# One load of 128 rows, its source read twice, in place of two loads of 64 rows, for the queries and keys of heads 12 to 63 in a fused attention and mixer kernel

## The chip, the core and the metric

The kernel runs on one core of one Trainium2 chip. The metric is device time in microseconds (us) of one execution, the median over runs. Engines go by the profile's names: PE (TensorE matmul), PEld (its weight loads), DVE (VectorE), ACT (ScalarE), POOL (GpSimd) and SP (SyncE, whose queue issues every transfer here). A *transfer* is one DMA instruction; it moves its rows as packets on the core's 16 DMA engines.

## The reference

Eight sequences of 576 tokens with 8 heads of width 64 go through block-causal attention (blocks of 64), and the result goes through a mixing layer of rank 32 along the sequence and a two-layer network of width 2048.

```
scores = scale * np.matmul(q, k.transpose(0, 1, 3, 2))     # (8, 8, 576, 576), scale = 1/8
mask = block_i >= block_j                                  # blocks of 64 positions
scores = np.where(mask, scores, -1000000000.0)
attn = softmax(scores)                                     # row sum + 1e-9
x = matmul(attn, v)                                        # heads side by side: (8, 576, 512)
h = x.T @ U @ V                                            # along the sequence, rank 32
u = x + h.T
out = u + np.maximum(u @ w_ch1, 0.0) @ w_ch2               # 512 -> 2048 -> 512
```

The kernel gets queries and keys as one array `qk` of shape (64, 64, 1152): for each of the 64 heads, 64 rows (the width), 576 columns of queries and then 576 of keys, so a row is 4,608 bytes and a head 288 KB.

## The kernel before, in words

**What runs over what.** The outer loop goes over 64 heads, head 0 to head 63. For each head the kernel loads q and k, forms the scores tile by tile (`softmax`, five row tiles of 64 or 128 queries), takes row maxima on DVE (L968) and exponentials on ACT (L979), normalises on POOL (L1005), transposes the weights on PE (L1038), splits them into high and low parts (ACT L1015, DVE L1057) and multiplies them with v on PE (L1097). After every second head `mix` applies the rank-32 layer and writes a piece of u to DRAM (L1166). The two-layer network of the first half of the weights (`ffn_chunk`: PE L465 and L488) is laid between the heads, one batch behind; after the last head comes the second half (`block_products`, PE L659).

**Queries and keys of a head.** `split_qk` loads into `raw`, a ring of two tiles of 128 x 1152, so head h uses `raw[h % 2]`. Up to head 11 only rows 0 to 63 are loaded (L868) and the scores are taken in plain fp32 (L950). From head FS = 12 on the scores are taken in two matmuls of fp32r (L954, L955), which need high and low parts, and both halves of `raw` get the same 64 rows: L868 fills rows 0 to 63, L873 fills rows 64 to 127. Then, in this order:

- ACT casts the queries of all 128 rows to q1 (L889), scales the keys in place (L892) and casts them to k1 (L894).
- POOL subtracts the low part of the queries in rows 64 to 127 (L896) and that of the keys in rows 0 to 63 into k2 (L900).
- SP copies rows 0 to 63 of q1 to q2 by a transfer (L904, 144 KB).
- PE takes the scores from q1, k1, q2, k2 (L954, L955).

`raw[h % 2]` is free for head h + 2 when L900 of head h is done, and the load of head h + 2 waits for that on SP.

**What sets the order.** A planner (`Plan.issue`) simulates the five engines as queues: each task has an engine, a cost in ns, a priority, and buffers that it reads and writes. It hands out ring buffers as they come free in its own simulated time and writes the instructions of every engine in the order in which the simulated engines took them up. A transfer costs its task's ns on SP, and its data count as there 3,000 ns later (`DL`). Before the change the load of heads 12 to 63 is entered at 1640 ns for its two transfers (L882). On the chip each engine works through that fixed order, and an instruction whose data are late holds up all that stands behind it on its engine.

**The other transfers.** All go through SP's one queue: v for two heads (`vr`, L913), pieces of u written (L1166) and read back for the network (`ur`, L440), its results (`o_d`, L499; read back at L452 and, in the second half, as `whole`), the weights (`st`, L372 and L387), and the final result (L756).

Of the kernel before, what the change touches and what calls it, by code (L numbers as in the profile page):

```python
# [16 lines left out]
P = 128  # L17
# [29 lines left out]
FS = 12  # L47
# [6 lines left out]
NEAR, DL = 130, 3000  # L54
# [83 lines left out]
class Plan:  # L138
# [8 lines left out]
    def add(self, engine, ns, prio, fn, reads=(), writes=(), hold=(), after=0, port=False):  # L147

        n = len(self.tasks)
        deps = set()  # L150
        for b in reads:
            deps.update(b.writers)
            b.readers.append(n)
        for b in hold:
            deps.update(b.readers, b.writers)
        for b in writes:
            deps.update(b.readers, b.writers)
            b.writers, b.readers = [n], []
        deps.discard(n)
        slots = {b for b in (*reads, *writes) if b.pool is not None}  # L160
        for b in slots:
            b.users += 1
        self.tasks.append((engine, ns, prio, fn, deps, after, slots, port or engine == "POOL"))
# [76 lines left out]
def _act(n, sbuf=False):  # L240
    return (93 if sbuf else 52) + 0.833 * n


def _dve(n):
    return 69 + 1.042 * n
# [9 lines left out]
def attention_then_mixer(  # L255
# [10 lines left out]
    nc = tc.nc  # L266
# [8 lines left out]
    add = plan.add  # L275

    def f32(ap):
        return ap.bitcast(F32)
# [531 lines left out]
    for r in raw_r:  # L810
# [3 lines left out]
        for x, fill in ((qi, 1.0), (ki, NEG)):  # L814
            nc.gpsimd.affine_select(
                out=x[:, :, 1, :], in_=x[:, :, 1, :], pattern=[[-1, 4], [0, 64]], compare_op=ALU.not_equal,
# [46 lines left out]
    def split_qk(h, pr):  # L863
        raw, q1, k1, q2, k2 = (r[h % 2] for r in (raw_r, q1_r, k1_r, q2_r, k2_r))

        def fetch():
            if h:
                nc.sync.dma_start(out=raw[0:64, :], in_=qk[h])  # L868
            else:
                for a in (S, 0):  # L870
                    nc.sync.dma_start(out=raw[0:64, a : a + S], in_=qk[h, :, a : a + S])
            if h >= FS:
                nc.sync.dma_start(out=raw[64:P, :], in_=qk[h])  # L873

        if h in (FS - 2, FS - 1):

            for n, (x, o) in enumerate(((q2, 0), (k2, S))):
                add(
                    "DVE", _dve(S) / 2, pr, lambda x=x, o=o: nc.vector.tensor_copy(x[64:P, :], raw[64:P, o : o + S]),
                    [raw], [x],  # L880
                )
        add("SP", 1640 if h >= FS else 820, pr, fetch, writes=[raw], after=DL)  # L882
        if h < FS:
            add(
                "ACT", _act(S, True), pr,
                lambda: nc.scalar.activation(raw[0:64, S : 2 * S], raw[0:64, S : 2 * S], AF.Copy, scale=SCALE), [raw], [raw],
            )
            return
        add("ACT", _act(S, True), pr, lambda: nc.scalar.copy(q1.ap, raw[:, 0:S]), [raw], [q1])  # L889
        add(  # L890
            "ACT", _act(S, True), pr,
            lambda: nc.scalar.activation(raw[:, S : 2 * S], raw[:, S : 2 * S], AF.Copy, scale=SCALE), [raw], [raw],  # L892
        )
        add("ACT", _act(S, True), pr, lambda: nc.scalar.copy(k1.ap, raw[:, S : 2 * S]), [raw], [k1])  # L894
        add(
            "POOL", 1380, pr, lambda: nc.gpsimd.tensor_sub(q1[64:P, :], raw[64:P, 0:S], f32(q1[64:P, :])),  # L896
            [raw, q1], [q1],
        )
        add(
            "POOL", 1380, pr, lambda: nc.gpsimd.tensor_sub(k2[0:64, :], raw[0:64, S : 2 * S], f32(k1[0:64, :])),  # L900
            [raw, k1], [k2],
        )

        add("SP", 600, pr, lambda: nc.sync.dma_start(out=f32(q2[0:64, :]), in_=f32(q1[0:64, :])), [q1], [q2], after=DL)  # L904
# [265 lines left out]

    wa = weight_tiles(wp, 0)
    split_qk(0, 0.0)
    split_v(0, 2.0)
    mixing_weights(MP)
    wab = weight_bufs()
    load_w1(lambda: wa, 0, wab, lambda n: WP0 + WP1 * n, (0,))
    for h in range(NH):
        pr = 1000.0 * h
        if h + 1 < NH:
            split_qk(h + 1, max(pr - LA, 1.0))  # L1180
        for g, tiles in ((1, (4, 3)), (0, (2, 1, 0))):
            for x in ((4,), (3,)) if g else ((2,), (1, 0)):
                softmax(h, x, pr + 10)
            normalise(h, tiles, pr + 10)
        for g in (1, 0):
            for part in range(2):
                transpose(h, g, part, pr + 20 + 10 * (1 - g))
            apply_v(h, g, pr + 30)
        if h + 1 < NH:
            split_v(h + 1, pr + 1000)  # L1190
        if h % 2 == 1:
            mix(h // 2, pr + 40)
        if h == min(WH, NH - 1):
            gate = Buf()
            gate.writers = [len(plan.tasks) - 1]
            load_w2(lambda: wa, 0, wab, lambda n: WPB + WP1 * n, [gate], ks=range(FH))
            load_w1(lambda: wa, 0, wab, lambda n: WP2 + WP3 * n, (1,), [gate])
            load_w2(lambda: wa, 0, wab, lambda n: WP4 + WP3 * (n - FH), [gate], ks=range(FH, FC))
# [59 lines left out]
```

## Time and profile before

| | |
|---|---|
| median of 3 runs | 1185.89 us (1184.37 to 1186.47) |
| profiled execution: time of the run | 1188.18 us |
| profiled execution: span | 1186.4 us |
| busy: PE, PEld | 1164.9 us (98%), 1132.5 us (95%) |
| busy: DVE, ACT, POOL | 937.9 us (79%), 775.6 us (65%), 455.2 us (38%) |
| transfers of q and k | 115 of 288 KB, 2 of 144 KB |
| busy share of the 16 DMA engines by SP's queue | 38.2% of the span |
| data moved | 130.36 MB, 110 GB/s on the mean |

The run's time is 1.8 us above the span, which begins with the first and ends with the last instruction of the program. A busy share is an average over stages: the heads last until about 635 us, and the network's second half follows. PE at 98% means that it has hardly any idle time; that its matmuls are at their peak is not said. The DMA share is a mean over 16 engines and does not tell how a transfer is divided among them.

### The profile page before, as it was taken

How to read it: one execution, taken by the hardware profiler on the slowest of the kernel's cores; microseconds unless marked ns; L12 is line 12 of the kernel's file. 1: busy time of each engine (PE TensorE's matmuls, PEld its weight loads, DVE VectorE, ACT ScalarE, POOL GpSimd, SP SyncE). 2: the span in 40 equal slices, each digit the busy share in tenths (PEclk: the TensorE clock that was granted, in tenths of full speed). 3: DMA queues.
4: the chain of work that ended last, by engine and by line, in shares of the span. 5: the costliest groups of instructions: out<-in, count | busy, mean ns of one | idle time of the engine just before them, and what ended most of it. 6: DMA issues, size and time to landing. Idle time of an engine off the chain costs nothing.

```text
span 1186.4 us, 25102 instructions
## 1 busy us (share of the span) xinstructions
PE 1164.9 (98%) x8988; PEld 1132.5 (95%) x8988; DVE 937.9 (79%) x2008; ACT 775.6 (65%) x1924; POOL 455.2 (38%) x582
## 2 busy tenths in 40 slices
PE   8989989999999999999999999999999999999998
PEld 7777989999999999999999999999999999999998
DVE  6898877878788877777877587326989889889887
ACT  7888878898888889988887352214544444444443
POOL 5656867675667676767664112110000000000000
PEclk9999999999999999999999999999999999999999
DMA  4455665544544444445431433211242142142121
GB/s 139 146 149 151 186 163 156 139 127 128 135 120 124 132 127 129 117 123 143 127 107 56 132 121 123 86 46 55 61 121 70 51 121 67 56 120 64 58 81 41
DMA packets 75868, 130.36 MB, mean 110 GB/s; under 512 B 8928, under 2 KB 52960, under 8 KB 75744
## 3 DMA queue, kind: packets, MB, share of 16 engines
q1 hardware_dynamic: 75744, 128.76, 38.2%
q8 instruction: 71, 1.16, 0.4%
q14 instruction: 53, 0.43, 0.1%
HBM read 91.57 MB, written 29.49 MB: 102 GB/s over the span
## 4 chain that ended last, share of the span: by engine, by line
PE 71%; DVE 4%; ACT 4%; issue 2%; DMA 0%; POOL 0%; SPq 0%; ACTq 0%; DVEq 0%; POOLq 0%
PE bb L659 30%; PE bf L465 9%; PE bf L488 8%; PE ba L1097 5%; PE ba L1038 5%; PE bg L488 4%; PE bg L465 4%; ACT p L979 1%; PE ba L955 1%; PE ba L954 1%; DVE mx L968 1%; PE ba L1136 1%; PE ba L1122 1%; PE bw L954 1%; PE bw L955 1%
## 5 line engine op out<-in xcount | busy, mean ns | idle before, releaser
L1005 POOL TENSOR_SCALAR p<-p,rv 128x192 f32<-128x192 f32 (+4 forms) x320 | 173.3, 556 | 162.3 <-DVE rv L996 68.3
L659 PE MATMUL bb<-hh,w1l 128*128 128x288 f32 x704 | 170.1, 295 | 0.0
L659 PE MATMUL bb<-hh,w1h 128*128 128x288 f32 x704 | 169.4, 295 | 0.0
L979 ACT ACTIVATE p<-ba,mx 128x448 f32<-128x448 f32 (+2 forms) x248 | 115.2, 469 | 20.6 <-DVE mx L968 15.5
L1038 PE MATMUL ba<-ident,p 128*128 128x128 f32 x768 | 122.2, 274 | 5.4 <-DVE xt L1105 1.6
L1057 DVE TENSOR_TENSOR pl<-ba,ph 128x512 fp32r<-128x512 f32 x216 | 114.2, 551 | 16.3 <-ACT ph L1015 13.2
L659 PE MATMUL bb<-hl,w1h 128*128 128x288 f32 x576 | 123.0, 295 | 0.1
L659 PEld LDWEIGHTS bb<-hh,w1l 128*128 128x128 f32 x704 | 123.0, 190 | 0.0
L659 PEld LDWEIGHTS bb<-hh,w1h 128*128 128x128 f32 x704 | 121.9, 188 | 0.0
L488 PE MATMUL bf<-hh,w2h 128*128 128x288 f32 x384 | 119.5, 311 | 0.1
L488 PE MATMUL bf<-hl,w2h 128*128 128x288 f32 x384 | 113.5, 295 | 0.0
L488 PE MATMUL bf<-hh,w2l 128*128 128x288 f32 x384 | 112.7, 293 | 0.0
L447 POOL TENSOR_TENSOR ul<-ur,uh 128x288 fp32r<-128x288 f32 x72 | 61.7, 887 | 123.6 <-PE bf L465 57.0
L1015 ACT CAST ph<-ba 128x512 fp32r<-128x512 f32 x216 | 99.8, 495 | 11.2 <-PE ba L1038 10.0
L613 ACT CAST hh<-hb 128x576 fp32r<-128x576 f32 x98 | 66.0, 673 | 60.5 <-PE bb L659 59.3
L968 DVE TENSOR_REDUCE mx<-ba 128x1 f32<-128x448 f32 (+3 forms) x248 | 94.2, 408 | 9.8 <-PE ba L955 6.7
L1038 PEld LDWEIGHTS ba<-ident,p 128*128 128x128 f32 x768 | 90.3, 141 | 11.4 <-issue 5.6
L659 PEld LDWEIGHTS bb<-hl,w1h 128*128 128x128 f32 x576 | 91.9, 188 | 0.4 <-DVE hl L614 0.4
L1097 PE MATMUL ba<-ph,vs 128*128 128x256 f32 (+3 forms) x432 | 89.0, 262 | 0.5 <-DVE xh L1127 0.2
L465 PE MATMUL bf<-uh,w1l 128*128 128x288 f32 x392 | 81.6, 304 | 0.0
L896 POOL TENSOR_TENSOR q<-raw,q 64x576 fp32r<-64x576 f32 x52 | 74.4, 1431 | 10.9 <-DMA vr<-in_v_dram 2.6
L900 POOL TENSOR_TENSOR k<-raw,k 64x576 fp32r<-64x576 f32 x52 | 74.5, 1432 | 4.1 <-ACT k L894 1.5
(172 smaller groups left out, 3366.8 us busy)
## 6 DMA issues: line engine op xcount, KB each, us to landing
raw<-in_qk_dram SPq DMA_DIRECT2D x115, 288.0 KB, 4.3
st<-in_w_dram SPq DMA_DIRECT2D x32, 512.0 KB, 3.8
o_d<-ot SPq DMA_DIRECT2D x72, 144.0 KB, 2.3
vr<-in_v_dram SPq DMA_DIRECT2D x32, 320.0 KB, 3.8
ur<-u_d SPq DMA_DIRECT2D x64, 144.0 KB, 2.9
whole<-o_d SPq DMA_DIRECT2D x32, 288.0 KB, 3.2
out_dram<-whole SPq DMA_DIRECT2D x32, 288.0 KB, 2.2
ur<-u_d SPq DMA_DIRECT2D x30, 288.0 KB, 3.5
```

The lines of the kernel that those rows point to most:

```text
L465: nc.tensor.matmul(ps[:, :T], w()[wn][:, k, fs], m[k].ap, start=(i == 0), stop=(i == len(ops) - 1))
L488: nc.tensor.matmul(ps[:, :T], w()[wn][:, f, ms], hs[f][x].ap, start=(i == 0), stop=(i == len(ops) - 1))
L659: nc.tensor.matmul(bank[:, i, :T], x()[:, w(k)], p.ap[:, k, :], start=first and n == 0, stop=last and n == len(ops) - 1)
L896: "POOL", 1380, pr, lambda: nc.gpsimd.tensor_sub(q1[64:P, :], raw[64:P, 0:S], f32(q1[64:P, :])),
L900: "POOL", 1380, pr, lambda: nc.gpsimd.tensor_sub(k2[0:64, :], raw[0:64, S : 2 * S], f32(k1[0:64, :])),
L968: lambda i=i, at=at: nc.vector.tensor_reduce(out=mx[: P if i else 64, i : i + 1], in_=view(i, at), op=ALU.max, axis=AX.XY if wide else AX. ...
L979: nc.scalar.activation(out.rearrange("p (j k) -> p j k", j=2) if wide else out, view(i, at), AF.Exp, bias=mx[:rows, i : i + 1], accum_out= ...
L1005: lambda x=x, rows=rows, i=i: nc.gpsimd.tensor_scalar(out=x, in0=x, scalar1=rv[:rows, i : i + 1], scalar2=1.0, op0=ALU.mult, op1=ALU.mult),
L1015: add("ACT", _act(n), pr, lambda: nc.scalar.copy(out(), inp()), reads, writes)
L1038: nc.tensor.transpose(out=bank[:, a : a + P], in_=pt_r[i][h % PB[i]][:, j * P : (j + 1) * P], identity=perm.ap)
L1057: "DVE", _dve(m), pr, lambda: nc.vector.tensor_sub(pl[:, low], bank[:, :m], f32(ph[:, low])), [bank, bh], [bl]
L1097: nc.tensor.matmul(bank[0 : c.stop, a:n], vs[:, j, c], x[:, _at(g, j)], start=(i == 0), stop=(i == len(ops) - 1))
```

## The change

For heads 12 to 63 the two transfers are replaced by one. Its destination is the whole tile `raw` (128 rows of 1152), and its source is the head's 64 rows with a leading step of size 2 and stride 0, so that they are read twice. The bytes read and written stay the same. The task's cost on SP, as the planner counts it, falls from 1640 to 820 ns. Below head 12 nothing changes. A line is added, so L873 and all lines after it stand one lower in the changed kernel (L889 becomes L890, L904 becomes L905), and the load of heads 12 to 63 is L869.

```
         def fetch():
-            if h:
+            if h >= FS:
+
+                nc.sync.dma_start(out=raw.ap, in_=qk[h].partition_broadcast(2))
+            elif h:
                 nc.sync.dma_start(out=raw[0:64, :], in_=qk[h])
             else:
                 for a in (S, 0):
                     nc.sync.dma_start(out=raw[0:64, a : a + S], in_=qk[h, :, a : a + S])
-            if h >= FS:
-                nc.sync.dma_start(out=raw[64:P, :], in_=qk[h])
...
-        add("SP", 1640 if h >= FS else 820, pr, fetch, writes=[raw], after=DL)
+        add("SP", 820, pr, fetch, writes=[raw], after=DL)
```

Since the planner counts a shorter task, it also lays out all engines a little differently from head 12 on. Two places show how much.

SP's queue at the first heads with the new load; `raw_141` is the tile of even heads and `raw_142` that of odd ones, `q_0_137` is q2 and `q_0_156` q1 of an even head, `vr` holds v, `st` weights, `u_d` and `ut` pieces of u. Before:

```order
L868 DMA raw_141<-in_qk_dram 64x1152
L873 DMA raw_141<-in_qk_dram 64x1152
L913 DMA vr_161<-in_v_dram 128x640
L387 DMA st_101<-in_w_dram 128x1024
L904 DMA q_0_137<-q_0_156 64x576
L868 DMA raw_142<-in_qk_dram 64x1152
L873 DMA raw_142<-in_qk_dram 64x1152
L868 DMA raw_141<-in_qk_dram 64x1152
L873 DMA raw_141<-in_qk_dram 64x1152
L1166 DMA u_d_75<-ut_181 128x576
```

With the change:

```order
L869 DMA raw_141<-in_qk_dram 128x1x1152
L914 DMA vr_161<-in_v_dram 128x640
L387 DMA st_101<-in_w_dram 128x1024
L905 DMA q_0_137<-q_0_156 64x576
L869 DMA raw_141<-in_qk_dram 128x1x1152
L869 DMA raw_142<-in_qk_dram 128x1x1152
L387 DMA st_100<-in_w_dram 128x1024
L1167 DMA u_d_75<-ut_181 128x576
```

Each pair of rows has become one row, whose destination now has three steps, 128 x 1 x 1152, to go with a source of 2 x 64 x 1152. The load of head 14 (the second into `raw_141`) has moved ahead of the load of head 13 (`raw_142`), and a load of weights (`st_100`) ahead of u's write.

PE at the scores of head 12: `bw` and `ba` are banks of the attention, `bf` one of the network, `v` and `t` the second product of `mix`. Before:

```order
L488 MATMUL bf_90<-hh,w2l_215 128x288
L488 MATMUL bf_90<-hl,w2h_214 128x288
L954 MATMUL bw<-k_0_158,q_0_156 128x288
L955 MATMUL bw<-k_0_139,q_0_137 128x288
L954 MATMUL bw<-k_0_158,q_0_156 128x288
L955 MATMUL bw<-k_0_139,q_0_137 128x288
L954 MATMUL ba_98<-k_0_158,q_0_156 128x448
```

With the change:

```order
L465 MATMUL bf_91<-ul_113,w1h_212 128x288
L1152 MATMUL ba_96<-v_183,t_0_178 128x288
L1152 MATMUL ba_97<-v_183,t_0_178 128x288
L955 MATMUL bw<-k_0_158,q_0_156 128x288
L956 MATMUL bw<-k_0_139,q_0_137 128x288
L955 MATMUL bw<-k_0_158,q_0_156 128x288
L956 MATMUL bw<-k_0_139,q_0_137 128x288
L488 MATMUL bf_90<-hh,w2h_214 128x288
```

The first scores of head 12 stood behind six matmuls of the network's second layer (L488) and now stand ahead of them; `mix`'s two matmuls (L1152), which stood twelve matmuls farther ahead, now come right before them. The same instructions are there; only which stands first is different, and so it is in many places up to the end of the heads.

## The prediction

> **What bounds the kernel now.** I read the page first, for the engine with the least idle time, and then the windows, for the stage in which the changed loads lie.
>
> ```profile
> span 1186.4 us, 25102 instructions
> ...
> PE 1164.9 (98%) x8988; PEld 1132.5 (95%) x8988; DVE 937.9 (79%) x2008; ACT 775.6 (65%) x1924; POOL 455.2 (38%) x582
> ...
> DMA packets 75868, 130.36 MB, mean 110 GB/s; under 512 B 8928, under 2 KB 52960, under 8 KB 75744
> ```
>
> ```profile
> 165.00:635.00 470.00, 467.14 (x3852) 456.00 (x3853) 369.27 (x996) 410.34 (x1156) 323.77 (x412) 1.00 0.47 127
> ```
>
> In the second row the first pair of numbers is PE's busy time: 467.14 of 470 us while the heads run. So PE is the bound, and all waits for loads together can't be worth more than 2.9 us in this stretch. What can be won is small; what can be lost has no such cap.
>
> Next the tile `raw`: the view of all that writes or reads it.
>
> ```profile
> L868 SPq DMA_DIRECT2D raw<-in_qk_dram x63: 465/471/1142, 2.0 to 613.8; - x63
> L873 SPq DMA_DIRECT2D raw<-in_qk_dram x52: 466/588/1816, 100.4 to 614.6; - x52
> L889 ACT CAST q<-raw x52: 656/674/690, 105.8 to 626.4; 128x576 fp32r<-128x576 f32 x52
> ...
>   DMA raw<-in_qk_dram: 4.4, 4
> ...
> DMA to landing us min/median/max: 2.8/4.3/8.1
> ```
>
> The casts of the 52 heads run from 105.8 to 626.4 us, so a head takes 520.6 / 51 = 10.2 us. A load lands 4.3 us after its issue, and only four waits of 4.4 us in all are put down to it. How early the loads are issued is read from the timeline: SP, then ACT, then POOL, around head 52.
>
> ```profile
> 504.17 0.47 SPq L868 DMA_DIRECT2D raw<-in_qk_dram  x1
> 504.70 0.59 SPq L873 DMA_DIRECT2D raw<-in_qk_dram  x1
> ...
> 521.79 0.47 SPq L868 DMA_DIRECT2D raw<-in_qk_dram  x1
> ```
>
> ```profile
> 515.05 0.68 ACT L889 CAST q<-raw 128x576 fp32r<-128x576 f32 x1 [0.78 <-PE ba L954]
> ```
>
> ```profile
> 520.33 1.43 POOL L900 TENSOR_TENSOR k<-raw,k 64x576 fp32r<-64x576 f32 x1
> ```
>
> Head 52's load is issued at 504.17 and 504.70 and its rows are first read at 515.05: 10.9 us after the first issue, of which about 5 are the two landings. POOL ends with the tile at 520.33 + 1.43 = 521.76, and SP issues the load of head 54 into it at 521.79. So loads go out as early as the two tiles allow, about one head ahead, and some 5.5 us of each are slack.
>
> **The change part by part.** *The second issue goes.* SP is freed of 52 x 0.588 = 30.6 us of issuing. SP is no bound: its longest waits are for others.
>
> ```profile
> SPq L868 <- POOL k L900: 114.0, 39, 7.6
> ```
>
> For 39 of the loads SP stood waiting for POOL's L900, 114 us in all. An issue that is shorter by half a microsecond only makes it wait longer. Worth: 0.
>
> *The order moves.* Bytes, matmuls and casts stay the same, and PE's stretch is full at 467.14 of 470. The regrouping of the two quoted places gains at most those 2.9 us, and I see no wait that it must add in the middle of the heads. I put it at 0, with 3 us to either side. One place counts only with the next part: the load of head 14 now stands ahead of that of head 13.
>
> *How the one load is divided among the DMA engines.* No transfer in the trace has a source with an outermost step of 2, so this must be bounded. First, what a transfer is now: the transfers of 105 to 630 us.
>
> ```profile
> DMA packets 33638, 70.18 MB, mean 134 GB/s; under 512 B 4828, under 2 KB 16860, under 8 KB 33571
> ## 3 DMA queue, kind: packets, MB, share of 16 engines
> q1 hardware_dynamic: 33571, 69.35, 49.0%
> ...
> raw<-in_qk_dram SPq DMA_DIRECT2D x102, 288.0 KB, 4.3
> vr<-in_v_dram SPq DMA_DIRECT2D x24, 320.0 KB, 3.9
> q<-q SPq DMA_DIRECT2D x51, 144.0 KB, 2.9
> u_d<-ut SPq DMA_DIRECT2D x25, 288.0 KB, 2.4
> o_d<-ot SPq DMA_DIRECT2D x43, 144.0 KB, 2.3
> ur<-u_d SPq DMA_DIRECT2D x43, 144.0 KB, 2.9
> st<-in_w_dram SPq DMA_DIRECT2D x4, 512.0 KB, 5.1
> ur<-o_d SPq DMA_DIRECT2D x8, 144.0 KB, 2.6
> ```
>
> The eight kinds are 300 transfers, and none has rows under 512 bytes (the shortest row is 288 x 4 = 1,152 bytes). The 4,828 packets under 512 bytes are thus 16.1 for each transfer: a closing packet from each of 16 parts. All these transfers have 64 or 128 rows as their outermost step on both sides, a multiple of 16, and each is cut into 16 equal lots of rows. The new source begins with a step of 2. If a transfer is cut along the outermost steps of both its sides, only 2 lots come out that fit both 2 and 128: each copy of the 64 rows becomes one lot, on one engine. If the 128 rows of the destination alone decide, it stays 16 lots of 8 rows. I take two lots, at 0.9: the trace has every transfer cut by its first step, and the new instruction is given three steps on both sides with the 2 outermost, while a cut by the destination alone is the special case. The Trainium skill, DMA: Bandwidth & Descriptors, section "Why a DMA increments its semaphore by 16 and not by 1", states this rule: the number of engines is the largest up to 16 that divides the outermost size of both patterns; the 16 closing packets agree, and no run here yet shows a 2. Its section "Rules for kernel authors" advises one transfer of 128 partitions over two of half the rows, which by itself speaks for this change, but in another row warns that a leading stride-0 broadcast of c copies is held to c engines.
>
> What a lot of 64 rows costs is read where nothing but rows of 4,608 bytes streams, 0.23 us within one load:
>
> ```profile
> DMA packets 19, 0.09 MB, mean 381 GB/s; under 512 B 0, under 2 KB 0, under 8 KB 19
> ## 3 DMA queue, kind: packets, MB, share of 16 engines
> q1 hardware_dynamic: 19, 0.09, 91.8%
> ```
>
> 0.918 x 16 x 0.23 us / 19 = 0.178 us a row on one engine, so 64 x 0.178 = 11.4 us for a load. That is the low end. The high end is the mean rate of the longer window: 49.0% of 16 engines over 525 us is 4,116 us for 69.35 MB, 16.85 GB/s for one engine; 64 x 4,608 bytes at that rate take 17.5 us. I take 11.4, since two streaming engines resemble the short window more than a mean over transfers that crowd all 16. The Trainium skill's page DMA: Bandwidth & Descriptors, section "Specifications", gives about 27 GiB/s for one engine, by which a load would be an estimated 10.2 us and the sum below about 62 us less; the row's 25.9 GB/s is measured here and decides.
>
> *What else these two engines must carry.* Every other transfer still has its sixteenth on each of them. In the same window raw is 102 x 294,912 bytes = 30.1 MB, the others 39.3 MB, 2.45 MB for each engine: 95 us at the streaming rate, 146 us at the mean rate. Middle: 120 us.
>
> *The sum.* The window of 525 us covers the heads with the new loads. The two engines then have 52 x 11.4 = 593 us of loads and 120 us of the rest, 713 us of work, where there are 525 us. The loads stand in one queue and can't be finished sooner, so the heads are stretched by 713 - 525 = 188 us (163 with the other traffic at 95 us, 214 at 146). The cover of 5.5 us a head doesn't help: it hides a late landing, not a lack of rate. Per head that is 13.9 us for 10.2.
>
> Is the queue ever empty? The load of head h + 2 goes out when POOL is done with head h, 6.7 us after its cast (521.79 - 515.05). By then the load of head h + 1 has some 5 of its 11.4 us to go. So mostly not. An exception is the start: the load of head 14 now lies ahead of head 13's, so head 13 comes 11.4 us later and, when it has landed, nothing is queued until POOL has finished with it: one hole of about 7 us.
>
> *What waits, and what stands behind it.* ACT's L889 waits for the load; behind it on ACT stand exponentials and casts for PE. The copy q2 (L904) is queued behind the next load on the two engines, and PE's L955 waits for it, with the network's matmuls behind. This has been seen once:
>
> ```profile
> 165.09 0.37 PE L955 MATMUL bw<-k,q 128*128 128x288 f32 x1 [1.72 <-DMA q<-q]
> ```
>
> ```profile
> 161.40:165.40 4.00, 2.28 (x19) 1.99 (x18) 2.66 (x7) 3.36 (x9) 0.86 (x1) 1.00 0.74 163
> 165.40:168.90 3.50, 3.50 (x17) 3.46 (x16) 2.37 (x7) 1.90 (x7) 0.53 (x1) 0.51 0.02 8
> ```
>
> PE waited 1.72 us for q2, was busy for 2.28 of 4.00 us, and in the next 3.5 us its granted clock was 0.51: such a wait costs up to 1.75 us more. With 3.7 us to spare in each head (13.9 - 10.2), one such loss hides. Where it delays POOL's L900 past the end of the load under way, the queue runs dry. Bounds: 0 to 1 us a head, 0 to 52 us; I take 10, nearer to the low end, as the lead of 5 us covers most.
>
> Together 188 + 7 + 10 = 205 us on the profiled execution's 1188.2 us: 1393. The median of the runs is 2.3 us below that execution, so 1391 us.
>
> **The rivals.** *Sixteen lots after all (not slower).* The destination's 128 rows decide, each engine gets 8 rows (1.4 us), and the load lands when the second of today's does. It decides if the closing packets are 16 a load. Then only the order moves: 1186 us, within 3. For it: every transfer so far has 16 parts. Chance 0.1, of it 0.05 within 0.2%, 0.03 faster, 0.02 slower; 0.2% (2.4 us) is about what a measurement of this kernel can tell from no change.
>
> *Two lots, but hidden by rate.* If successive loads went to different pairs of engines, the rate would not bind and only the lag would count. From the fixed part of a load of four rows an engine,
>
> ```profile
> DMA to landing us min/median/max: 3.5/3.9/8.1
> ```
>
> 3.9 - 4 x 0.178 = 3.2 us, a load lands 11.4 + 3.2 = 14.6 us after its issue; with 6.7 us to the tile's release two heads take 21.3 us, 10.7 each: 51 x 0.45 = 23 us, about 1209. Nothing in the trace shows engines being alternated. The Trainium skill, in the section on the semaphore named above, has the lowest-numbered engines taken each time, which would exclude this; no row here tells engines apart. Chance 0.05.
>
> *Two lots and slower still.* If rows take more than 0.23 us each because two engines draw at one source, or the loads never overlap and each head takes the full 21.3 us: 51 x 11.1 = 566, about 1752. Against it: the load of the next head is out about one head ahead. Chance 0.05.
>
> **How the numbers follow.** Two lots on fixed engines has 0.8, and 1391 is its sum. Its low end is the 163 us alone, with up to 9 us off for work at the ends of the stretch: 1340. Its high end takes rows at 0.226 us, halfway between 0.178 and 17.5 / 64 = 0.274: 14.5 us a load, 52 x 14.5 + 146 - 525 = 375, and the 52 us of empty queue: 427 on 1186, 1610. Outside are sixteen lots, the alternating engines and the slowest case, 0.2 together. Slower: 0.8 + 0.05 + 0.05 + 0.02 = 0.92; same 0.05; faster 0.03.
>
> **What would show it.** Two lots: the page's packets under 512 bytes fall from 8928 by 52 x 30 to 7368 (16 lots: 8096, one transfer less for each head); raw's 52 loads land 14 us or more after issue; the cast L890 waits for DMA on most heads; casts run from about 106 to 830 us, 13.9 a head; PE's busy time stays near 1165 us and its share falls to some 84%, with granted clock below 1.00 in many windows of the heads; after the heads the second half takes as long as now. I am wrong if the closing packets stay 16 a load, if landing stays under 6 us, or if the heads stretch although the loads land before their casts.

## The result and the profile after

The changed kernel takes 1405.12 us (median of 5 runs, 1404.54 to 1406.98) for 1186.06 us before (5 runs). The ratio is 1.1853 with an interval of 1.1835 to 1.187: it is slower by 219 us. 1391 us was forecast, in a range of 1340 to 1610.

The page of the changed kernel, the same rows as before the change:

```profile
span 1403.3 us, 25019 instructions
...
PE 1217.2 (87%) x8988; PEld 1181.6 (84%) x8988; DVE 944.6 (67%) x2008; ACT 785.2 (56%) x1924; POOL 455.1 (32%) x582
...
DMA packets 74307, 130.35 MB, mean 93 GB/s; under 512 B 7368, under 2 KB 51400, under 8 KB 74184
```

The packets under 512 bytes are 7368: two closing packets for each of the 52 loads. PE has 8988 matmuls as before and is now idle for 186 us of its span (21.5 us before). It is also busy 52 us longer (1217.2 for 1164.9): the same work at a lower granted clock, as the window over the heads shows in its third number from the end:

```profile
165.00:845.00 680.00, 535.07 (x4002) 519.01 (x4001) 396.51 (x1041) 437.54 (x1204) 338.66 (x429) 0.90 0.29 95
```

The clock is 0.90 on the mean there (1.00 before), and PE is busy for 535 of 680 us.

The tile `raw`, in the view of all that writes or reads it: the one load, the cast that waits for it, and the sum of the waits put down to it.

```profile
L869 SPq DMA_DIRECT2D raw<-in_qk_dram x52: 525/540/650, 100.3 to 825.3; - x52
L890 ACT CAST q<-raw x52: 662/671/677, 115.7 to 841.7; 128x576 fp32r<-128x576 f32 x52
...
  DMA raw<-in_qk_dram: 100.5, 31
```

The casts run from 115.7 to 841.7 us, 726.0 / 51 = 14.2 us a head for 10.2. That is where the whole loss lies: the first cast is 9.9 us later than before (115.7 for 105.8), the casts are stretched by 205.4 us, and after the last cast there are 561.6 us for 560.0. Together 216.9 us, the difference of the two spans.

Five microseconds in which only one load streams (678.5 to 683.5 us), by the DMA view, show the two engines:

```profile
DMA packets 60, 0.26 MB, mean 52 GB/s; under 512 B 2, under 2 KB 2, under 8 KB 60
## 3 DMA queue, kind: packets, MB, share of 16 engines
q1 hardware_dynamic: 60, 0.26, 12.7%
```

12.7% of 16 engines is two engines without a pause, at 52 GB/s together. Two of the packets are closing ones; 0.127 x 16 x 5 us / 58 = 0.175 us a row.

The same view over the heads, 105 to 842 us:

```profile
q1 hardware_dynamic: 31850, 69.53, 28.3%
```

A share of 28.3% looks like slack, as it is a mean over 16. In 737 us it is 3,337 us of engine time. 51 loads of 64 rows at 0.175 us on two engines are 1,142 us of that; if the other 2,195 us are spread evenly, each engine has 137 us of them. The two engines then work 571 + 137 = 708 of 737 us, 96% of the time (an estimate from these rows); the other fourteen 19%.

The packet records in the trace, which have a start and a length for each packet but no engine, can be counted directly. Between 105 and 842 us fewer than two packets of SP's queue are under way for 15.8 us, 2% of the time, and exactly two for 69% of it. Before the change (105 to 630 us) it was fewer than two for 222 of 525 us, and exactly two for 1%. So the two engines can both be at work for at most 98% of the stretch, and the 96% of the sum is close to that.

What waits, in the view of the waits:

```profile
POOL p L1006 <- DVE rv L997: 139.8, 51, 9.1
PE bw L956 <- DMA q<-q: 119.2, 33, 7.8
ACT q L890 <- DMA raw<-in_qk_dram: 95.9, 27, 20.5
```

Row two is PE in front of the scores, waiting for the copy q2, which stands behind a load in SP's queue; row three is ACT waiting for the load. The chain that ended last has 32% of its time in transfers:

```profile
PE 52%; DMA 32%; ACT 6%; DVE 5%; issue 3%; POOL 2%; SPq 0%; ACTq 0%; POOLq 0%; DVEq 0%
PE bb L659 25%; DMA q<-q 16%; DMA raw<-in_qk_dram 14%; PE bf L488 5%; PE bf L465 5%; PE bg L465 3%; PE bg L488 3%; PE ba L1039 3%; PE ba L1098 2%; ACT p L980 2%; PE bw L956 1%; DVE mx L969 1%; DMA ur<-u_d 1%; DMA u_d<-ut 1%; PE ba L956 1%
```

### The profile page after: what moved, and what is told of

The parts are those of the page before. It is cut to its first block, busy times and chain, and to the rows that moved or that the text cites. A ratio compares the mean times of both kernels' runs of the same rounds, so it can differ in the third digit from the quotient of the medians.

```text
span 1403.3 us, 25019 instructions
## 1 busy us (share of the span) xinstructions
PE 1217.2 (87%) x8988; PEld 1181.6 (84%) x8988; DVE 944.6 (67%) x2008; ACT 785.2 (56%) x1924; POOL 455.1 (32%) x582
## 2 busy tenths in 40 slices
DMA packets 74307, 130.35 MB, mean 93 GB/s; under 512 B 7368, under 2 KB 51400, under 8 KB 74184
## 4 chain that ended last, share of the span: by engine, by line
PE 52%; DMA 32%; ACT 6%; DVE 5%; issue 3%; POOL 2%; SPq 0%; ACTq 0%; POOLq 0%; DVEq 0%
PE bb L659 25%; DMA q<-q 16%; DMA raw<-in_qk_dram 14%; PE bf L488 5%; PE bf L465 5%; PE bg L465 3%; PE bg L488 3%; PE ba L1039 3%; PE ba L1098 2%; ACT p L980 2%; PE bw L956 1%; DVE mx L969 1%; DMA ur<-u_d 1%; DMA u_d<-ut 1%; PE ba L956 1%
## 5 line engine op out<-in xcount | busy, mean ns | idle before, releaser
L956 PE MATMUL bw<-k,q 128*128 128x288 f32 x104 | 38.6, 381 | 121.1 <-DMA q<-q 119.2
L956 PEld LDWEIGHTS bw<-k,q 128*128 128x128 f32 x104 | 23.8, 228 | 128.0 <-issue 75.5
L1039 PE MATMUL ba<-ident,p 128*128 128x128 f32 x768 | 129.1, 288 | 2.1 <-POOL p L1006 1.6
L488 PE MATMUL bf<-hh,w2h 128*128 128x288 f32 x392 | 125.7, 321 | 0.0
L980 ACT ACTIVATE p<-ba,mx 128x448 f32<-128x448 f32 (+2 forms) x248 | 114.7, 467 | 18.2 <-DVE mx L969 16.0
L890 ACT CAST q<-raw 128x576 fp32r<-128x576 f32 x52 | 34.9, 672 | 158.7 <-DMA raw<-in_qk_dram 95.9
L488 PE MATMUL bf<-hl,w2h 128*128 128x288 f32 x392 | 119.7, 305 | 0.0
L488 PE MATMUL bf<-hh,w2l 128*128 128x288 f32 x392 | 119.5, 305 | 0.0
L969 DVE TENSOR_REDUCE mx<-bw 128x1 f32<-128x576 f32 x64 | 48.1, 752 | 84.3 <-PE bw L956 78.0
L1039 PEld LDWEIGHTS ba<-ident,p 128*128 128x128 f32 x768 | 99.3, 150 | 4.9 <-POOL p L1006 2.5
L1098 PE MATMUL ba<-ph,vs 128*128 128x256 f32 (+3 forms) x432 | 92.9, 267 | 10.3 <-DVE pl L1058 10.3
```

The source lines that it names most:

```text
L488: nc.tensor.matmul(ps[:, :T], w()[wn][:, f, ms], hs[f][x].ap, start=(i == 0), stop=(i == len(ops) - 1))
L956: nc.tensor.matmul(o, q2[:, qs], k2[:, ks], start=False, stop=True)
L969: lambda i=i, at=at: nc.vector.tensor_reduce(out=mx[: P if i else 64, i : i + 1], in_=view(i, at), op=ALU.max, axis=AX.XY if wide else AX. ...
L980: nc.scalar.activation(out.rearrange("p (j k) -> p j k", j=2) if wide else out, view(i, at), AF.Exp, bias=mx[:rows, i : i + 1], accum_out= ...
L1039: nc.tensor.transpose(out=bank[:, a : a + P], in_=pt_r[i][h % PB[i]][:, j * P : (j + 1) * P], identity=perm.ap)
L1098: nc.tensor.matmul(bank[0 : c.stop, a:n], vs[:, j, c], x[:, _at(g, j)], start=(i == 0), stop=(i == len(ops) - 1))
```

## The experiments

My theory: the load is cut into two lots because its source begins with a step of 2, and two engines then have more work in a head than PE has. Rivals: reading the same rows twice is slow; a source of three steps is slow; the planner's new order is what costs; or not the rate but the late landing of each load. Each ratio is to the kernel before, run on the same chip.

### Is it the number of lots? Four layouts of the source

All four keep the order, the bytes, and one load of 128 rows of the changed kernel. An extra array in DRAM holds each head's 64 rows twice, and only how its rows stand differs.

```
+    qk2 = np.concatenate([qk, qk], axis=1)                       # one_step: 128 rows
...
+    qk2 = np.zeros((b * h, G, R + 1, 2 * s), qk.dtype)           # gap_G: G groups of R = 128 / G rows
+    qk2[:, :, 0:R, :] = np.concatenate([qk, qk], axis=1).reshape(b * h, G, R, 2 * s)
...
-                nc.sync.dma_start(out=raw.ap, in_=qk[h].partition_broadcast(2))
+                nc.sync.dma_start(out=raw.ap, in_=qk2[h])                 # one_step
+                nc.sync.dma_start(out=raw.ap, in_=qk2[h, :, 0:R, :])      # gap_G
```

**one_step.**

> The array of queries and keys stands twice in DRAM, so that the one load of 128 rows reads 128 rows in one step (outermost 128 on both sides); order and bytes as in the changed kernel. Two lots as the cause (mine): 16 closing packets a load again, packets under 512 bytes 8096, time back at 1183 to 1189 us. If one transfer for both halves or the planner's new order were the cause: it stays near 1405 us.

Measured: 1185.16 us, ratio 1.0003 (0.9994 to 1.0013).

**gap_2.**

> The rows stand twice in DRAM with one empty row between the halves: outermost step 2 as in the change, but no row is read twice. Two lots as the cause: 2 closing packets a load (7368 under 512 bytes) and 1395 to 1415 us. If reading the same rows twice were what is slow: about 1186 us.

Measured: 1406.95 us, ratio 1.1875 (1.1857 to 1.1893).

**gap_4.**

> The same 128 rows in 4 groups of 32 with an empty row after each: outermost step 4. Mine: 4 closing packets a load (7472 under 512 bytes), 32 rows x 0.19 = 6.1 us on each of four engines, with 1.8 to 2.8 us of other traffic 8 to 9 us a head, under the 10.2 of PE: the rate no longer binds, the landing (6.1 + 3.2 = 9.3 us) just fits the 10.9 us lead; 1186 to 1215 us. If any source of three steps is slow, or lots are 16 or 2 whatever the count: 1405 or 1186.

Measured: 1256.34 us, ratio 1.059 (1.055 to 1.0631).

**gap_16.**

> The same 128 rows in 16 groups of 8 with an empty row after each: three steps as in the change, outermost step 16. Mine (the count of the outermost step decides, not that there are three): 16 closing packets a load, 8096 under 512 bytes, 1183 to 1189 us. If three steps are slow by themselves: near 1405 us.

Measured: 1187.99 us, ratio 1.0024 (1.0014 to 1.0034).

The packets on the page of each kernel, and the casts in the view of its tile `raw`, in this order:

```profile
DMA packets 75035, 130.35 MB, mean 110 GB/s; under 512 B 8096, under 2 KB 52128, under 8 KB 74912
```

```profile
L891 ACT CAST q<-raw x52: 661/673/698, 106.2 to 621.7; 128x576 fp32r<-128x576 f32 x52
...
DMA to landing us min/median/max: 2.8/3.8/6.2
```

```profile
DMA packets 74307, 130.35 MB, mean 93 GB/s; under 512 B 7368, under 2 KB 51400, under 8 KB 74184
```

```profile
L891 ACT CAST q<-raw x52: 660/671/692, 116.5 to 841.9; 128x576 fp32r<-128x576 f32 x52
```

```profile
DMA packets 74411, 130.35 MB, mean 105 GB/s; under 512 B 7472, under 2 KB 51504, under 8 KB 74288
```

```profile
L891 ACT CAST q<-raw x52: 660/674/697, 110.7 to 683.2; 128x576 fp32r<-128x576 f32 x52
```

```profile
DMA packets 75035, 130.35 MB, mean 110 GB/s; under 512 B 8096, under 2 KB 52128, under 8 KB 74912
```

```profile
L891 ACT CAST q<-raw x52: 661/673/696, 107.7 to 624.9; 128x576 fp32r<-128x576 f32 x52
...
DMA to landing us min/median/max: 2.9/5.3/7.6
```

The closing packets are 16, 2, 4 and 16 a load, so the outermost step of the source sets the lots. gap_2 reads no row twice and is as slow as the change: re-reading is not the cause. gap_16 has three steps and is within 0.3% of before: three steps aren't either. one_step makes one transfer out of two with 16 lots and gains nothing, as PE is full. gap_4 has the lots that I expected but not the time: 71 us slower than before, where I had put 0 to 30.

### Is it the order?

**order_only** enters 820 ns but issues the two old transfers.

```
-                nc.sync.dma_start(out=raw.ap, in_=qk[h].partition_broadcast(2))
+                nc.sync.dma_start(out=raw[0:64, :], in_=qk[h])
+                nc.sync.dma_start(out=raw[64:P, :], in_=qk[h])
```

> The planner's cost of 820 ns as in the change, but the two old transfers of 64 rows: the new order alone. Mine: the order is worth nothing beyond 3 us, 1183 to 1189 us. If the order made the loss: towards 1405 us.

Measured: 1185.41 us, ratio 1.0004 (0.9995 to 1.0013).

**old_cost** keeps the broadcast load and enters 1640 ns.

```
-        add("SP", 820, pr, fetch, writes=[raw], after=DL)
+        add("SP", 1640 if h >= FS else 820, pr, fetch, writes=[raw], after=DL)
```

> The one broadcast load, but entered at the old 1640 ns, so the order is that of before but for the dropped instruction; head 13's load stands ahead of head 14's again. Mine: the rate binds, 1395 to 1410 us, some 7 us of the hole at the start gone. If the new order is what the slow load suffers from: well under 1390 us.

Measured: 1403.91 us, ratio 1.1836 (1.1817 to 1.1855). With either kind of load the order is worth nothing that these runs can tell.

### Rate or lag?

**even_heads** keeps the broadcast load for heads 12, 14 and so on, and two transfers for odd heads.

```
-            if h >= FS:
+            if h >= FS and h % 2:
+                nc.sync.dma_start(out=raw[0:64, :], in_=qk[h])
+                nc.sync.dma_start(out=raw[64:P, :], in_=qk[h])
+            elif h >= FS:
                 nc.sync.dma_start(out=raw.ap, in_=qk[h].partition_broadcast(2))
```

> The broadcast load for even heads alone, odd heads keep two transfers of 64 rows (order of the change). Rate as the cause: for two heads the two engines carry 64 + 8 rows at 0.19 = 13.7 us and 4 to 5.6 us of other traffic, 18 to 19 us, less than the 20.4 us of PE: nearly hidden, 1186 to 1215 us. If each late load cost its own lag (about 219 / 52 = 4.2 us a head): half the loss stays, about 1295 us.

Measured: 1287.89 us, ratio 1.0869 (1.0846 to 1.0892). I was wrong here and the lag was right: half of the loads cost 103 us, though the two engines have time. Twice that would be 206 of the 219 us, so by this run alone the lag could pass for the whole loss. By the DMA view from 115 to 727 us,

```profile
q1 hardware_dynamic: 32385, 68.57, 38.2%
```

that is 3,741 us of engine time in 612 us; 26 loads on two engines at 0.175 us a row are 582 us, the rest is 197 us an engine, and the two work for 291 + 197 = 488 of 612 us, 80%. By the count of packet records fewer than two are under way for 111 of the 612 us, 18%. What binds is seen in one turn of the even tile, in the timeline of SP, ACT and POOL:

```profile
586.00 0.56 SPq L871 DMA_DIRECT2D raw<-in_qk_dram  x1
...
608.64 0.57 SPq L871 DMA_DIRECT2D raw<-in_qk_dram  x1
```

```profile
601.79 0.67 ACT L892 CAST q<-raw 128x576 fp32r<-128x576 f32 x1 [1.47 <-DMA raw<-in_qk_dram]
```

```profile
607.19 1.43 POOL L903 TENSOR_TENSOR k<-raw,k 64x576 fp32r<-64x576 f32 x1
```

The load goes out at 586.00, ACT waits for it and casts at 601.79, POOL releases the tile at 608.62, and the next load goes out at 608.64: 15.8 us from issue to cast and 6.8 us from cast to release, one after the other. This turn covers two heads and takes 22.6 us, where PE needs 20.4. The cover of 5.5 us that I had read off before is used up by a load whose rows are there only 15.8 us after its issue, some 10 us later than the two old transfers (about 5 us).

**three_tiles** gives `raw` a third tile.

```
-    raw_r = ring(ap, 2, [P, 2 * S], F32, "raw")
+    raw_r = ring(ap, 3, [P, 2 * S], F32, "raw")
...
-        raw, q1, k1, q2, k2 = (r[h % 2] for r in (raw_r, q1_r, k1_r, q2_r, k2_r))
+        raw, q1, k1, q2, k2 = (r[h % len(r)] for r in (raw_r, q1_r, k1_r, q2_r, k2_r))
...
-        raw = raw_r[h % 2]
+        raw = raw_r[h % len(raw_r)]
```

> The broadcast load with three tiles raw in place of two, so that a load goes out one head earlier. Rate as the cause: only the holes in the queue close, the two engines still need some 13 us a head; 1345 to 1395 us. If the lag of a load were the cause: a lead longer by a head hides it, 1186 to 1215 us.

Measured: 1395.72 us, ratio 1.1777 (1.1761 to 1.1794), just above the upper end of what I gave the rate and far from what I gave the lag. The waits for its tiles `raw` and q in their views, the waits of PE, and its DMA share from 105 to 830 us:

```profile
  DMA raw<-in_qk_dram: 33.5, 6
```

```profile
  DMA q<-q: 168.1, 46
```

```profile
PE bw L956 <- DMA q<-q: 118.9, 30, 8.4
```

```profile
q1 hardware_dynamic: 32312, 70.19, 28.9%
```

For q the changed kernel with two tiles has, in the same view,

```profile
  DMA q<-q: 151.8, 47
```

The waits for the load fall from 100.5 to 33.5 us, so the lag of the load is now mostly hidden, and yet the time hardly falls. The waits for the copy q2 stay: 168.1 us for 151.8 in the view of q, and for PE itself 118.9 us for 119.2. By the same sum as above (0.289 x 16 x 725 = 3,352 us, of it 1,142 for 51 loads, 138 an engine for the rest) the two engines work for 709 of 725 us, 98%. By the count of packet records fewer than two are under way for 14 of the 725 us. The casts come every 14.3 us.

### Is it the copy q2 in line behind the loads?

In four kernels q2 is issued by ACT, and the profile lists its packets as a queue of their own (q10). The edit is the same in all:

```
-        add("SP", 600, pr, lambda: nc.sync.dma_start(out=f32(q2[0:64, :]), in_=f32(q1[0:64, :])), [q1], [q2], after=DL)
+        add("ACT", 60, pr, lambda: nc.scalar.dma_start(out=f32(q2[0:64, :]), in_=f32(q1[0:64, :])), [q1], [q2], after=DL)
```

**act_two_loads**, on top of order_only:

> Control: two transfers of 64 rows a head, order of the change, and the copy q2 issued by ACT's queue in place of SP's. No two-lot load. Every theory: 1183 to 1200 us; what it differs from order_only is the price of the other queue.

Measured: 1189.72 us, ratio 1.0039 (1.0025 to 1.0054). The other queue costs some 4 us.

**act_even_heads**:

> even_heads with q2 issued by ACT's queue, so that it doesn't stand behind a load in SP's rings. If the loss of even_heads (103 us) is the copy waiting in line behind the load: 1186 to 1225 us. If it is the late landing of the load itself or the rate: 1260 to 1295 us.

Measured: 1308.88 us, ratio 1.1025 (1.0991 to 1.106): above both ranges, and 21 us slower than even_heads.

**act_gap_4**:

> gap_4 (4 lots) with q2 issued by ACT's queue. If the 71 us of gap_4 are the copy in line behind the load: 1186 to 1205 us. If they are the load's own lag or rate: 1240 to 1260 us.

Measured: 1232.96 us, ratio 1.0403 (1.0347 to 1.0458): between the two ranges.

**act_broadcast**:

> The changed kernel with q2 issued by ACT's queue. If the rate of two engines is a floor of its own: 52 x 12.1 = 631 us of loads and at least some 45 us of other packets in place of 525 us, so no less than 1337 and up to 1390 us. If the copy in line behind the loads is the whole loss: under 1260 us. If neither matters beside the load's lag: 1395 to 1410 us.

Measured: 1398.81 us, ratio 1.1798 (1.1777 to 1.1818). That is 9 us above what I gave the rate and inside what I gave the load's lag, so the time alone doesn't decide between them. By the count of packet records fewer than two are under way for 14 of the 730 us from 105 to 835, so here too the two engines have hardly a pause. The waits for its tiles q and `raw` in their views:

```profile
  DMA q<-q: 18.3, 23
```

```profile
  DMA raw<-in_qk_dram: 111.8, 28
```

The waits for q2 fall from 151.8 to 18.3 us, and the time by 6 us. ACT waits for the load as before, and PE now waits for exponentials (L980), which stand on ACT behind the cast that waits for the load. In the changed kernel and here:

```profile
PE ba L1039 <- ACT p L980: 19.8, 1, 19.8
```

```profile
PE ba L1039 <- ACT p L980: 65.6, 15, 20.1
```

With three_tiles this makes a pair: take away either wait, for the load or for q2, and the time hardly moves, since both stand at the same two full engines. A kernel with both at once, three tiles and q2 on ACT's queue, was not run.

Where the engines aren't full it is otherwise. In gap_4 fewer than four packets are under way for 110 of the 578 us from 105 to 683, so its four engines have time; there q2's place behind the load is worth 23 us of the 71, 28 with the control's 4 to 5 us added. Where the other 43 us come from is not settled. In even_heads q2's place is worth nothing; that kernel even gets 21 us slower, and why is not settled either.

## Why the prediction was right, and what was off

- **PE is full, so nothing can be won.** Shown by one_step: 16 lots and one issue less give 1.0003.
- **The order moves, worth 0.** Shown by order_only and old_cost.
- **Two lots.** Right; 7368 as forecast, and the four layouts show that the outermost step decides. The Trainium skill (DMA: Bandwidth & Descriptors, section "Why a DMA increments its semaphore by 16 and not by 1") gives this rule; 2, 4 and 16 lots agree with it.
- **11.4 us a load, at 0.178 us a row.** The lone stream has 0.175.
- **The rate of two engines is the bound: 13.9 us a head.** Measured 14.2, and by the sum over the profile and the count of its packets the engines are busy for 96 to 98% of the time. That an earlier issue or a free q2 doesn't help (1396 and 1399 us) is what a full engine predicts. The stretch of 525 us was to grow by 188 + 17 us; the casts grew by 205.4. That the two agree to the microsecond is partly luck: the 188 us had 120 us of other traffic, where the sum above has 137, and the parts of the 17 us are not confirmed, as the next two points say. The 9.9 us before the first cast, the wait for the first load at the start of the line, I hadn't counted; they are most of the 14 us by which the forecast was low.
- **One hole of 7 us for head 14's load ahead of head 13's.** The hole is there but its price is not confirmed. By the packet records no row of q and k is under way from 145.7 to 159.9 us, yet other transfers fill most of that: fewer than two packets are under way for 5.3 us of it. old_cost has the old order there, and its 1403.91 us can't be told from the 1405.12 us of the change.
- **10 us for an empty queue and a lower clock.** Not separated. The clock did fall to 0.90 over the heads, and PE's 52 us of longer work fit into its idle time; whether they cost anything at the end was not tried. Here the list of signs was off: it had PE's busy time near 1165 us and its share at 84%, and they are 1217.2 us and 87%. Of its other signs, ACT waited for a load before 27 of the 52 casts, hardly most, and the profile of the change has no landing times to check the 14 us by.
- **The rival "two lots, but hidden by rate", 1209 us.** Its condition isn't met: four rows of q and k are under way at once for less than 1 us of the 737, where loads on changing pairs of engines would show that whenever two loads overlap. But its price was mis-sized: with half of the loads, where the rate doesn't bind, the time is already 1288 us. I took a turn of the tile at 14.6 + 6.7 = 21.3 us. The quoted turn has 22.6, and the mean of even_heads, with its casts from 114.6 to 727.3 us, is 24.0 for two heads. A transfer that lands late also stops ACT's queue and all behind it; that this makes up the difference is argued, not shown. What failed there is the first half of "it hides a late landing, not a lack of rate": 5.5 us do not hide a landing that is 10 us later. The same omission made me expect 1186 to 1215 us of gap_4 and even_heads.

So the loss has two layers. A load on two engines lands too late for two tiles (103 us for every other head); and with every head the two engines are full, which keeps a head at 14.1 to 14.3 us also with a third tile or with q2 on the other queue. The lag at the price of even_heads would come to nearly the same loss; it is the time staying when the wait for the load goes, and the count of packets, that speak for the rate.

## What to carry to other kernels

Count the lots of a transfer before its bytes: a source that begins with a broadcast of 2 was moved by 2 engines here, and merging two transfers into one in that way cost 219 us, where a merger with 16 lots cost nothing. Look for such a transfer in its closing packets and in a DMA share that stays near 2/16, as the mean share over 16 engines (28.3% here) hides two that are full. When a load gets longer, check its rate against the period of the loop and its lag against the cover, separately; either can bind.

## What the runs showed that I had not expected

With the two engines full, SP itself is held up. In the changed kernel the issue of v that often follows it on SP (`vr`, L914; L913 before) takes 1.8 us on the median and up to 5.8, where it took 0.34 before:

```profile
L914 SPq DMA_DIRECT2D vr<-in_v_dram x32: 327/1818/5781, 2.6 to 809.1; - x32
```

```profile
L913 SPq DMA_DIRECT2D vr<-in_v_dram x32: 328/339/1021, 2.6 to 596.2; - x32
```

How often depends on the order (old_cost: 0.39 us on the median, up to 7.3), and in even_heads and gap_4, where the engines have time, no such issue takes over 0.6 us. What holds it up isn't shown. And a load of 128 rows in 16 groups lands in 5.3 us, in one step in 3.8 us, both with 16 closing packets (gap_16, one_step).
